# Two pairs of layer-norm statistics back to back, one square root for the first pair, late transposes moved behind the paired chunks

## The chip, the cores and the metric

The kernel runs on one core of a Trainium2 chip. The metric is device time in microseconds (us). A core has five engines with a program order each: TensorE (PE, matrix products and transposes), VectorE (DVE), ScalarE (ACT), GpSimd (POOL) and SyncE (SP, here a queue that issues transfers). Transfers run on 16 DMA engines. Engines wait for each other by semaphores.

## What is computed

Two layers, each an attention block (A) and a dense block (B), each with a residual, over 2048 tokens of width 1024, in bf16:

```python
x = A_x                                   # [1, 2048, 1024]
for _ in range(2):
    x = x + A(layernorm(x), wqkv, wo)     # 32 heads of 32; each token sees 8 tokens, 2 apart
    x = x + B(layernorm(x), w1, b1, w2, b2)   # 1024 -> 3584, gelu, -> 1024
```

Layer norm subtracts a token's mean and divides by the square root of its variance plus 1e-5.

## The kernel before

Tokens are cut into four groups of 512, a group into four tiles of 128 tokens. With two layers there are eight stages n = 0 to 7. For each stage, `gen_qkv` makes queries, keys and values, chunk by chunk (`qkv_chunk`, 8 matmuls of 128x512 for each of 8 chunks); DVE makes the products of queries and keys (`new_prod`), the softmax and the weighted values (`av`, which writes chunk c of `oT`); `gen_wo` multiplies by wo, and `gen_ffn1` and `gen_ffn2` are block B. Of `wo`, the accumulation runs over the chunks c = 0 to 7 of `oT`. PE takes its work in the order of the program. The wrapper `InOrder` (L81) does the same for another engine while its flag `on` is set: `vec` is DVE, `act` is ACT, `sp` is SP. Where the flag is off, a scheduler places the instructions.

The change lies at the very start, in stage 0. A normalised tile has to reach PE transposed (`xnT`, features on the partitions). For the first four tiles, x[0] to x[3], this goes two ways:

- Tiles 0 and 1: PE transposes the raw x (`banks[0]`, `banks[1]`; ACT copies each bank into `raw` in two parts, features k = 0, 1 first and k = 2 to 7 later). `queries_of_raw` multiplies the raw tiles by the query weights, in rows of 7 chunks for each k from 0 to 7 (matmuls of 128x258), and mean and standard deviation are worked in afterwards: `spread_stats` (after row k = 2) turns them into rows on PE, and `finish(c)` corrects each chunk. For the keys and values, the same two tiles are also normalised on DVE (`norm(0)`, `norm(1)`, list `first_early`) and transposed by DMA on the SP queue.
- Tiles 2 and 3: DVE makes statistics (`stats`: two BATCH_NORM_STATS2 and one BATCH_NORM_AGGREGATE), ACT the root (`root`), DVE the reciprocal and the normalised tile (`norm`). PE transposes them (`first_late`, `transpose_on_pe`) between the matmuls of `queries_of_raw`, both into the same PSUM bank, and ACT copies the bank to `xnT` in between.

Behind `queries_of_raw`, `gen_qkv` sends the SP queue on. In this order stand there: the two DMA transposes of `first_early`; the first half of the key weights wk, x[6], the second half of wk, x[7], x[8] to x[11]; then, tile by tile, the DMA transposes of `ln_early`, which normalises x[4] to x[9] on DVE with the root on ACT (`ln_stats` with `root=True`). x[10] and x[11] get their statistics on ACT (`ln_stats_ahead`, an Identity activation with a sum, then a Square activation with a sum, L213 and L214); here `act.on` is only set for g == 2, and the `act` wrapper keeps their order among themselves alone. The stage then needs wk for its key chunks, which DVE multiplies with the queries as they come.

Of the kernel before, what the change touches and what calls it, by code (L numbers as in the profile page):

```python
# [8 lines left out]
ACT = mybir.ActivationFunctionType  # L9
# [8 lines left out]
def kernel(  # L18
# [18 lines left out]
    P = 128  # L37
# [13 lines left out]
    KD = D // P  # L51
# [26 lines left out]
    def acc_tile():  # L78
        return psum.tile([P, T], F32, name="acc", bufs=8)
# [23 lines left out]
    vec, act, pool, sp = InOrder(nc.vector), InOrder(nc.scalar), InOrder(nc.gpsimd), InOrder(nc.sync)  # L103
# [6 lines left out]
    def pe(inst):  # L110
        if last_pe[0] is not None:
            dep_order(inst, last_pe[0], "PE program order")
        last_pe[0] = inst
        return inst

    def mm(*args, **kwargs):
        return pe(nc.tensor.matmul(*args, **kwargs))  # L117
# [37 lines left out]
    eps_t = const.tile([P, 1], F32, name="eps_t")  # L155
# [71 lines left out]
    def transpose_on_pe(xn, out, bank, parts=(0, KD)):  # L227
        pst = bank[:].bitcast(BF16).rearrange("p (k t) -> p k t", t=P)
        for k in range(KD):
            pe(nc.tensor.transpose(pst[:, k, :], xn[:, k * P:(k + 1) * P], ident[:]))  # L230
        copy_transposed(out, bank, parts)

    def copy_transposed(out, bank, parts):
        pst = bank[:].bitcast(BF16).rearrange("p (k t) -> p k t", t=P)
        for k0, k1 in zip(parts[:-1], parts[1:]):
            act.copy(out[:, k0:k1, :], pst[:, k0:k1, :])
# [8 lines left out]
    first_early, first_late = [], []  # L245
    NT = 2 * P

    def ln_first():

        xnT = xa[0] = new_xnT()  # L250
        vec.on = act.on = True
        raw = attp.tile([P, KD, NT + 2], BF16, name="vT", bufs=2)
        vec.memset(raw[:, :, NT:NT + 2], 1.0)
        mv = lnp.tile([P, 4, 2], F32, name="mvs", bufs=1)
        std = lnp.tile([P, 4], F32, name="stds", bufs=1)
        rstd = lnp.tile([P, 4], F32, name="rstds", bufs=1)
        less = lnp.tile([P, 2], F32, name="lesses", bufs=1)

        def stats(tt):
            st6 = lnp.tile([P, 2, 6], F32, name="stats")  # L260
            for h in range(2):
                vec.bn_stats(st6[:, h, :], x[tt][:, h * HALF:(h + 1) * HALF])
            vec.bn_aggr(mv[:, tt, :], st6[:])

        def root(tt):
            act.activation(std[:, tt:tt + 1], mv[:, tt, 1:2], ACT.Sqrt, bias=eps_t[:])

        def norm(tt, out):
            if tt > 1:
                vec.reciprocal(rstd[:, tt:tt + 1], std[:, tt:tt + 1])  # L270
            vec.tensor_scalar(out=out, in0=x[tt][:], scalar1=mv[:, tt, 0:1], scalar2=rstd[:, tt:tt + 1],
                              op0=ALU.subtract, op1=ALU.mult)
            return out

        warm_ps = acc_tile()
        warm_up(7, warm_ps)
        banks = [acc_tile(), acc_tile()]
        for tt in range(2):
            transpose_on_pe(x[tt], raw[:, :, tt * P:(tt + 1) * P], banks[tt], (0, 2))
        warm_up(2, warm_ps)  # L280
        stats(0)
        root(0)
        copy_transposed(raw[:, :, 0:P], banks[0], (2, KD))
        stats(1)
        root(1)
        copy_transposed(raw[:, :, P:NT], banks[1], (2, KD))
        vec.tensor_scalar(out=less[:], in0=mv[:, 0:2, 0], scalar1=-1.0, scalar2=None, op0=ALU.mult)
        vec.reciprocal(rstd[:, 0:2], std[:, 0:2])
        by_token = iop.tile([P, 4, P], F32, name="tmp")

        def spread_stats(bank):
            for i, column in enumerate((less[:, 0:1], less[:, 1:2], rstd[:, 0:1], rstd[:, 1:2])):
                pe(nc.tensor.transpose(bank[:, i * P:(i + 1) * P], column.to_broadcast([P, P]), identf[:]))
            rows = by_token[:].rearrange("p i t -> p (i t)")
            act.copy(rows, bank[:])
            return rows[:, 0:NT], rows[:, NT:2 * NT]

        xn01 = bigp.tile([P, 2, D], BF16, name="big")
        first_early.append((norm(0, xn01[:, 0, :]), xnT[:, 0, :, :]))

        def rest():
            for tt in range(2, 4):
                stats(tt)
                root(tt)
                if tt == 2:
                    first_early.append((norm(1, xn01[:, 1, :]), xnT[:, 1, :, :]))
                xn = lnp.tile([P, D], BF16, name="xn", bufs=3)
                norm(tt, xn[:])
                first_late.append((xn, xnT[:, tt, :, :]))

        return raw, spread_stats, rest

    def queries_of_raw(wq, qT):
        raw, spread_stats, rest = st.pop("raw")
        first = {}

        def row(c, k):
            if k == 0:
                first[c] = acc_tile()
            mm(first[c][:, 0:NT + 2], lhsT=wq[k // (KD // 2)][:, k % (KD // 2), c::NCH], rhs=raw[:, k, :],  # L320
               start=(k == 0), stop=(k == KD - 1), skip_group_check=True)

        part = attp.tile([P, NCH, NT], F32, name="abc")

        def finish(c):
            vec.scalar_tensor_tensor(out=part[:, c, :], in0=less, scalar=first[c][:, NT:NT + 1], in1=first[c][:, 0:NT],
                                     op0=ALU.mult, op1=ALU.add)
            pool.tensor_tensor(out=qT[:, c, 0:NT], in0=part[:, c, :], in1=rstd, op=ALU.mult)

        for k in range(KD):  # L330
            for c in range(7):
                row(c, k)
                if (k, c) == (0, 6):
                    bank = acc_tile()
                if (k, c) == (2, 6):
                    less, rstd = spread_stats(bank)
                    rest()
                if (k, c) == (5, 3):
                    transpose_on_pe(*first_late.pop(0), bank)
                if (k, c) == (7, 6):  # L340
                    transpose_on_pe(*first_late.pop(0), bank, (0, KD // 2, KD))
        act.on = False
        act.hold()
        for c in range(7):
            finish(c)
        for k in range(KD):
            row(7, k)
        vec.on = False
        return lambda: finish(7)

    def new_xnT(pool=None):
        return (pool or xnp).tile([P, NTT, KD, P], BF16, name="xnT")
# [38 lines left out]
    def gen_qkv(n, defer=False, qk_pool=None, v_late=False, qk_next=None, v_first=False, mix=0):  # L391
# [29 lines left out]
        if n == 0:  # L421
            last = queries_of_raw(wq, qT)
            for xn, out in first_early:
                sp.dma_start_transpose(out, xn.rearrange("s (k p) -> s k p", p=P))
            wk = load_qkv(1, lambda: load_x(1, 2, 3))
            load_x(1, 3, 4)
            load_x(2)
            early_tiles = ln_early((1, None), (2, qk_next))
            for tt in range(2):
                next(early_tiles)  # L430
                if tt == 0:
                    last()
            wv = load_qkv(2)
            for _ in early_tiles:
                pass
            vec.hold()
            sp.on = False
            sp.hold()
# [203 lines left out]
    def warm_up(count, ps):  # L642
        for _ in range(count):
            mm(ps[:], lhsT=warm[:], rhs=warm[:].unsqueeze(1).to_broadcast([P, NTT, P]), start=True, stop=True)
# [62 lines left out]

    pool.on = True
    st["raw"] = ln_first()
    first = build_constants()  # L710
    with tc.tile_pool(name="early", bufs=1) as early:
# [63 lines left out]
```

## Time and profile before

| | |
|---|---|
| median of 4 runs | 1229.23 us (1229.04 to 1229.52) |
| the profiled execution | 1229.28 us, span 1227.5 us |
| PE busy | 1220.2 us, 99% of the span |
| DVE / ACT / POOL busy | 865.5 / 314.6 / 121.5 us |
| granted PE clock | 1.0 |

The profile is of one execution. Its page gives busy times; a timeline gives start, length, engine, line, operation, "written<-read" and shapes, with the idle time ahead of a row and what ended it in square brackets. Neighbouring rows of one kind are merged ("x2"). Line 92 is the wrapper `InOrder`, line 117 is `mm`, so rows are told apart by their tiles: `stds` and `mvs` belong to tiles 0 to 3, `std` and `mv` to `ln_early`, `vT` is also the buffer of `raw` at the start, `big` holds the normalised tiles 0 and 1 there. PEld rows are weight loads, which run ahead of their matmuls. SPq rows are the times that the SP queue spent on issuing, not the transfer itself. The chain of waits follows the work that ended last back in time, and shows start, length and what.

### The profile page before, as it was taken

The page shows a single profiled execution, that of the slowest core. Times are in us where ns is not written, and L with a number is a line of the kernel's source. Part 1 is how long each engine was busy: PE and PEld are TensorE (multiplying, and loading weights), DVE is VectorE, ACT ScalarE, POOL GpSimd, SP SyncE. Part 2 cuts the span into 40 slices and gives each one's busy share as a digit, 9 for nine tenths or more (in the row PEclk, how much of TensorE's full clock was granted, in tenths as well). Part 3 has the DMA queues.
Part 4 walks back from the last instruction along what each step waited for, and adds up shares of the span by engine and source line. Part 5 has one row for each costly group of instructions (what it writes and reads, how often), then busy time and mean ns, then how long its engine had stood idle before and what let it go on. Part 6 is the DMA issues. An engine that isn't in the chain of part 4 may idle for free.

```text
span 1227.5 us, 13975 instructions
## 1 busy us (share of the span) xinstructions
PE 1220.2 (99%) x5719; PEld 632.0 (51%) x5769; DVE 865.5 (71%) x926; ACT 314.6 (26%) x498; POOL 121.5 (10%) x217
## 2 busy tenths in 40 slices
PE   9999999999999999999999999999999999999998
PEld 7666544456444554446544465444654444444444
DVE  7999897998898999375993759937598797011001
ACT  4443253014410243202431024310234001300310
POOL 2430006010101101100001000000000001000000
PEclk9999999999999999999999999999999999999999
DMA  9976665765738645856557565486664568446541
GB/s 309 266 220 194 181 198 174 202 186 190 226 121 254 185 151 162 238 172 172 167 158 224 172 171 185 155 218 198 171 204 148 186 191 210 149 160 193 157 136 50
DMA packets 225824, 227.18 MB, mean 185 GB/s; under 512 B 74000, under 2 KB 192928, under 8 KB 223712
## 3 DMA queue, kind: packets, MB, share of 16 engines
q1 hardware_dynamic: 216304, 208.17, 56.5%
q0 software_dynamic: 8880, 17.07, 4.2%
q8 instruction: 45, 0.74, 0.3%
q10 hardware_dynamic: 576, 1.05, 0.2%
q14 instruction: 19, 0.16, 0.0%
HBM read 189.01 MB, written 4.19 MB: 157 GB/s over the span
## 4 chain that ended last, share of the span: by engine, by line
PE 90%; DVE 7%; DMA 1%; issue 1%; SPq 0%; ACT 0%; POOL 0%; DVEq 0%
PE acc L117 90%; DVE big L92 5%; DMA x<-in_A_x_dram 1%; DVE stats L92 1%; DVE e L92 0%; DMA abc<-a 0%; DVE tmp L92 0%; DVE oT L92 0%; SPq L92 0%; POOL abc L92 0%; DVE xn L92 0%; DVE qT L92 0%; DVE a L92 0%; DVE z L92 0%; ACT vT L92 0%
## 5 line engine op out<-in xcount | busy, mean ns | idle before, releaser
L117 PE MATMUL acc<-xnT,wt 128*128 128x512 bf16 (+1 forms) x3328 | 712.9, 377 | 0.1
L117 PEld LDWEIGHTS <-wt 128*128 128x128 bf16 x3392 | 400.7, 119 | 318.8 <-issue 0.9
L117 PE MATMUL acc<-wt,hT 128*128 128x512 bf16 (+1 forms) x1780 | 386.0, 376 | 2.1
L117 PEld LDWEIGHTS <-hT 128*128 128x128 bf16 x1820 | 178.0, 98 | 209.1
L92 DVE TENSOR_TENSOR big<-big 128x2048 bf16<-128x2048 bf16 (+2 forms) x185 | 244.8, 1351 | 2.2
L92 ACT ACTIVATE hT<-acc,b1T 128x512 bf16<-128x512 f32 x224 | 151.7, 688 | 323.3 <-PE acc L117 323.2
L92 DVE TENSOR_TENSOR big<-qT,kT 128x4096 bf16<-128x4096 bf16 x64 | 143.8, 2283 | 37.4 <-ACT kT L92 35.9
L92 DVE TENSOR_TENSOR big<-abc,vT 128x4096 bf16<-128x4096 bf16 x64 | 144.6, 2282 | 11.2 <-DMA abc<-a 7.2
L92 DVE TENSOR_TENSOR tmp<-acc,b2bc 128x512 f32<-128x512 f32 x56 | 38.6, 689 | 154.0 <-PE acc L117 150.9
L92 ACT CAST qT<-acc 128x512 bf16<-128x512 f32 (+1 forms) x64 | 35.5, 558 | 275.4 <-PE acc L117 275.3
L117 PE MATMUL acc<-wt,oT 128*128 128x512 bf16 x440 | 97.5, 379 | 0.4
L92 DVE BATCH_NORM_STATS2 stats<-x 128x6 f32<-128x512 bf16 x116 | 77.3, 680 | 5.0 <-DMA x<-in_A_x_dram 4.0
L117 PEld LDWEIGHTS <-oT 128*128 128x128 bf16 x448 | 43.8, 98 | 52.9 <-issue 0.2
L92 DVE TENSOR_TENSOR x<-acc,big 128x512 bf16<-128x512 f32 (+1 forms) x9 | 5.7, 632 | 90.1 <-PE acc L117 90.0
L92 POOL TENSOR_TENSOR rstd<-mv,eps_t 128x1 f32<-128x1 f32 x48 | 14.6, 304 | 500.2 <-DVE mv L92 500.2
L92 ACT CAST vT<-acc 128x512 bf16<-128x512 f32 x64 | 37.4, 585 | 100.7 <-PE acc L117 100.7
L92 ACT CAST kT<-acc 128x512 bf16<-128x512 f32 x64 | 37.0, 584 | 59.7 <-PE acc L117 59.7
L92 DVE TENSOR_TENSOR x<-acc,x 128x512 bf16<-128x512 f32 x64 | 42.9, 670 | 5.2 <-PE acc L117 4.8
L92 DVE TENSOR_SCALAR xn<-x,mv,rstd 128x1024 bf16<-128x1024 bf16 x48 | 26.2, 545 | 19.9 <-POOL rstd L92 19.9
L92 DVE TENSOR_TENSOR x<-tmp,x 128x512 bf16<-128x512 f32 x56 | 38.6, 689 | 1.4
L92 POOL DMA_DIRECT2D big<-big x24 | 13.3, 564 | 212.3 <-DVE big L92 212.2
L92 ACT ACT_TABLE_LOAD x17 | 21.8, 1283 | 43.7 <-DVE e L92 30.7
(82 smaller groups left out, 303.4 us busy)
## 6 DMA issues: line engine op xcount, KB each, us to landing
wt<-in_B_w_dram SPq DMA_DIRECT2D x56, 1024.0 KB, 5.8
wt<-in_B_w_dram SPq DMA_DIRECT2D x64, 896.0 KB, 5.0
wt<-in_A_wqkv_dram SPq DMA_DIRECT2D x46, 1024.0 KB, 5.7
wt<-in_A_wo_dram SPq DMA_DIRECT2D x16, 1024.0 KB, 5.1
abc<-a POOLq DMA_DIRECT2D x32, 256.0 KB, 4.7
big<-big POOLq DMA_DIRECT2D x24, 256.0 KB, 3.9
out_dram<-x SPq DMA_DIRECT2D x31, 128.0 KB, 1.8
x<-in_A_x_dram SPq DMA_DIRECT2D x14, 256.0 KB, 5.9
```

Of the source, the lines that this page charges most:

```text
L92: inst = f(*args, **kwargs)
L117: return pe(nc.tensor.matmul(*args, **kwargs))
```

## The change

In ACT's order, both late parts of the raw copies now stand ahead of the roots, and one root covers tiles 0 and 1. In DVE's order, the statistics of tiles 2 and 3 follow directly on the reciprocal of tiles 0 and 1; then come norm(2), norm(3), norm(0), norm(1). On PE, the transposes of tile 2 move from behind chunk 3 of row k = 5 to the end of row k = 6; those of tile 3 stay at the end of row k = 7. The order of the SP queue is the same.

```diff
-        def root(tt):
-            act.activation(std[:, tt:tt + 1], mv[:, tt, 1:2], ACT.Sqrt, bias=eps_t[:])
+        def root(t0, t1):
+            act.activation(std[:, t0:t1], mv[:, t0:t1, 1], ACT.Sqrt, bias=eps_t[:])
...
-        stats(0)
-        root(0)
-        copy_transposed(raw[:, :, 0:P], banks[0], (2, KD))
-        stats(1)
-        root(1)
-        copy_transposed(raw[:, :, P:NT], banks[1], (2, KD))
+        for tt in range(2):
+            copy_transposed(raw[:, :, tt * P:(tt + 1) * P], banks[tt], (2, KD))
+            stats(tt)
+        root(0, 2)
...
-        first_early.append((norm(0, xn01[:, 0, :]), xnT[:, 0, :, :]))
 
         def rest():
             for tt in range(2, 4):
                 stats(tt)
-                root(tt)
-                if tt == 2:
-                    first_early.append((norm(1, xn01[:, 1, :]), xnT[:, 1, :, :]))
+                root(tt, tt + 1)
+            for tt in range(2, 4):
                 xn = lnp.tile([P, D], BF16, name="xn", bufs=3)
                 norm(tt, xn[:])
                 first_late.append((xn, xnT[:, tt, :, :]))
+            for tt in range(2):
+                first_early.append((norm(tt, xn01[:, tt, :]), xnT[:, tt, :, :]))
...
-                if (k, c) == (5, 3):
+                if (k, c) == (6, 6):
                     transpose_on_pe(*first_late.pop(0), bank)
                 if (k, c) == (7, 6):
                     transpose_on_pe(*first_late.pop(0), bank, (0, KD // 2, KD))
```

## The prediction

> **What bounds the kernel now.** I read the engine shares, the chain of waits, then the timelines of the first 30 us and of 121 to 124 us.
>
> The page's engine shares:
>
> ```profile
> PE 1220.2 (99%) x5719; PEld 632.0 (51%) x5769; DVE 865.5 (71%) x926; ACT 314.6 (26%) x498; POOL 121.5 (10%) x217
> ```
>
> TensorE (PE) is busy for 99% of the span, but that is an average. Two windows of the chain of waits say more, one up to 24 us, one around 122 us (start, length, what):
>
> ```profile
> 12.71 0.29 SPq L92
> ...
> 13.05 0.57 SPq L92
> ...
> 14.70 8.37 DMA x<-in_A_x_dram
> ...
> 23.09 1.30 DVE stats L92 x2
> ```
>
> ```profile
> 114.34 7.88 DVE big L92 x6
> 122.22 0.68 DVE oT L92 x2
> 122.90 10.79 PE acc L117 x49
> ```
>
> Until 122.90 us the chain does not run through PE. It runs through VectorE (DVE), and before 23.09 us through SyncE's DMA queue (SP): DVE waits there for x[7], issued at 14.70 and landed at 23.07. From 122.90 on, the chain is PE to the end of the span. So a delay of DVE is lost time once it exceeds DVE's slack at 122.9, and a delay of PE is lost time in full. What was the SP queue doing before 13.05?
>
> ```profile
> 8.79 4.21 SPq L92 DMA_TRANSPOSE xnT<-big  x2
> 13.05 0.57 SPq L92 DMA_DIRECT2D wt<-in_A_wqkv_dram  x1
> 13.68 0.49 SPq L92 DMA_DIRECT2D x<-in_A_x_dram  x1
> 14.22 0.43 SPq L92 DMA_DIRECT2D wt<-in_A_wqkv_dram  x1
> 35.33 2.64 SPq L92 DMA_TRANSPOSE xnT<-qT  x2
> ```
>
> The transposes of tiles 0 and 1 stand ahead of both halves of wk (13.05, 14.22) and of x[6], x[7]. They go out when norm(0) and norm(1) are done, and the change moves those two norms to the end of DVE's first block. That decides the case.
>
> **Part by part.**
>
> *Front of PE (gain).* ScalarE's (ACT) rows:
>
> ```profile
> 6.11 0.79 ACT L92 COPY vT<-acc 128x768 bf16<-128x768 bf16 x1
> 7.26 0.29 ACT L92 ACTIVATE stds<-mvs,eps_t 128x1 f32<-128x1 f32 x1 [0.36 <-DVE mvs L92]
> 7.46 0.78 ACT L92 COPY vT<-acc 128x768 bf16<-128x768 bf16 x1
> 8.29 0.93 PE L117 MATMUL acc<-vT,wt 128*128 128x258 bf16 x7 [0.30 <-ACT vT L92]
> ```
>
> Each copy stands behind a root (the first root at 5.91), and PE waits for the second. In the changed order the copies run at 5.91 to 6.70 and 6.60 to 7.38, so row k=2 starts when the 14 matmuls before it are through (6.07 + 14 x 0.11 = 7.61): 0.67 us earlier than 8.29. The paired root falls at 7.29, the reciprocal at 7.63 instead of 7.59: nothing.
>
> *Late transposes (cost on PE).* They stood 17 matmuls apart and now stand 7 apart (0.77 us), in the same bank. The ACT copy that frees the bank takes 0.99 us and starts 0.2 after the first set, so the second set waits about 0.4. With the wait of 0.16 that this place had before, PE reaches the first 128x256 query about 0.3 earlier (15.33 to 15.0).
>
> *DVE's block.* Now: reciprocal 7.63, statistics of 2 and 3, norms 2, 3, 0, 1. x[2] landed at 7.98 (issue 1.80 plus 6.2), so statistics run from 8.00, 1.28 + 0.21 each with the rows' overlaps, to 10.93. Then norm 2 from 10.99, 3 from 11.64, 0 from 12.09, 1 from 12.54 to 13.09 (0.55 each, 0.45 where one follows another, the reciprocals between). Before, the block ended at 13.81: DVE gains 0.7, of which two removed waits for a root are 0.32 + 0.36.
>
> *The SP queue (the large cost).* norm(0) ends at 12.64 instead of 8.34. The first transpose goes out at 12.69 instead of 8.79 and nothing passes it. Two of them cost at least 2 x 1.24 plus 0.05; the quiet pair at 35.33 held the queue for 2.64 and released it at 38.01, the pair at 8.79 for 4.21, because the second one took 2.78 while loads were under way. In the changed kernel no load is queued ahead of them but x[5], which landed at 13.17, so I take the quiet pair: the first half of wk goes out at 12.69 + 2.73 (35.33 to 38.06) = 15.4 instead of 13.05. Landing times in the DMA issue rows (last number, us to landing), for the loads at 14.22, 38.06 and 118.34 (the one at 13.05 has 5.9):
>
> ```profile
> wt<-in_A_wqkv_dram SPq DMA_DIRECT2D x1, 1024.0 KB, 8.2
> wt<-in_A_wqkv_dram SPq DMA_DIRECT2D x1, 1024.0 KB, 5.7
> wt<-in_A_wo_dram SPq DMA_DIRECT2D x1, 1024.0 KB, 5.0
> ```
>
> After a quiet pair it is 5.7: its first half lands at 15.4 + 5.7 = 21.1 instead of 13.05 + 5.9 = 19.0, and everything behind it in the queue keeps its distance. So the delay d of wk's second half and of x[7] is 2.1. Bounds: 1.3 (nothing under 5.0 us is seen for 1 MB, and the queue cannot be free before 15.2) and 3.7 (the second transpose takes 2.78 again). I take 2.1, because the pair at 35.33 is the nearest row: two transposes, then 1 MB loads, nothing large in flight ahead of them.
>
> *What d does to PE.* wk's second half lands at 22.4, needed by the fifth matmul of the first key chunk: queries from 15.33, 64 x 0.109, then 4 x 0.216 = 23.17. Slack 0.75. With d = 2.1 it lands at 24.5: PE stands still about 1.7 us and is 1.4 later than before from there; the 0.3 gained at the front is swallowed.
>
> *What d does to DVE.* x[7]'s statistics start at 25.2 instead of 23.09: 2.1 later. The 0.7 gained is swallowed by the same wait.
>
> *One more instruction on ACT.* Outside the edit, the scheduler places one root differently. In the changed program's order, the Square activation of x[10] (from ln_stats_ahead, L214) stands ahead of the root of tile x[9]; now it stands behind:
>
> ```profile
> 28.33 0.19 ACT L92 ACTIVATION_READ_ACCUMULATOR xn<-x 128x1 f32 x1
> 28.75 0.29 ACT L92 ACTIVATE std<-mv,eps_t 128x1 f32<-128x1 f32 x1 [0.23 <-DVE std L92]
> 28.95 1.14 ACT L92 ACTIVATE xn<-x,less 128x1024 bf16<-128x1024 bf16 x1
> ```
>
> With ACT's earlier roots also 2.1 later (26.70 to 28.80), the chain is root 0.2, kT cast 0.47, sum 0.96, read 0.22, Square 1.06, read 0.09: the root starts at 31.8, ends at 32.1. DVE's reciprocal wants it at 29.24 + 2.1 = 31.34. Cost 0.8 on DVE; bounds 0 (ACT caught up) and 1.2 (all of Square plus its read). DVE is then 2.9 late, and its block of products up to 122.9 runs without a gap that could take this back: its one wait after that, 1.99 before 88.61, is for weights that DVE itself makes.
>
> *Where both meet.* wo's first chunk needs oT of c = 7, written at 122.90; PE loads those weights at 123.82 (load at 123.39 is the sixth, plus 2 x 0.215). DVE slack 0.9. PE alone asks for +1.4; DVE for 2.9 - 0.9 = 2.0. They run side by side, so the later one counts: +2.0. Behind it the chain is PE alone, with nothing to win back.
>
> Sum: 1229.28 (profiled execution: span 1227.5 plus 1.8 around it; the median is 1229.23, 0.05 below) + 2.0 = 1231.3.
>
> *A rule on standing still.* The profile's PEclk row shows full clock in every slice, and no wait of PE after 4.3 us exceeds 0.5; mine are 1.7 at 23 us and 0.6 at 123. At the very start the row of warm-up matmuls shows 7 in 3.17 us, 0.427 apart, twice the later 0.216. If a stop of 1.7 brought that back for such a stretch, PE would lose half of 3.2, 1.6 more, and be at +3.0 instead of +2.0.
> The Trainium skill, "TensorE: Matmul & The Clock Gate", Part 1 ("What's actually happening"), puts the fall to half clock at an idle window of about 3.4 us; by that rule a stop of 1.7 costs nothing more and the sum stays +2.0.
>
> **Rivals.** 0.2% is 2.46 us, about what a measurement of this kernel can tell from no change.
>
> (1) *The transpose pair stays slow.* If it holds the queue for 4.21, d is 3.7: DVE 3.7 + 0.8 - 0.9 = +3.6, PE 3.7 - 0.75 = +2.95, time 1232.9. For it: four of the five pairs in the first 50 us that I looked at have a slow second transpose. Against: in each of these a load was in flight ahead. It passes 0.2% from d = 2.6.
>
> (2) *Half clock after the stop*: +3.0, 1232.3, as above.
>
> (3) *ACT catches up*: no 0.8; PE's +1.4 decides, 1230.7.
>
> (4) *Not slower.* The loads land when they did: then PE keeps its 0.3 and DVE its 0.7, and the time is 1229.0. It needs d below 0.6, against the queue's own times (15.2 at the earliest, against 13.05), and what it wins is under 0.2% all the same. A gain over 0.2% has no row behind it: PE's waits before 14 us add up to 1.3.
>
> **Numbers.** Forecast (+1.6 to +2.46) 0.38; (3) and other mild cases, d down to 1.3, 0.16; (4) 0.04; (1) 0.22; (2) 0.07; a further late transfer that I do not see, slower, 0.11; faster by over 0.2%, 0.02. So faster 0.02, same 0.58, slower 0.40. Range: low end d = 1.3 without ACT's cost, where PE decides with 1.3 - 0.75 = +0.55, less the 0.25 by which the runs shown lie off their middle; high end rival (1) with the same 0.1 to 0.2 more: 1229.6 to 1233.0.
>
> **What would show it.** First transpose on SP near 12.7, wk's halves issued near 15.4 and 16.5; PE waiting 1.7 near 22.9 for a wt landing; DVE waiting 2 to 4 us in all for x[6] and x[7], statistics of x[7] near 25.2; root of x[9] near 31.8 behind Square; PE waiting about 0.6 for oT near 125. It is wrong if wk goes out before 14.5 or after 17, if PE does not wait for oT, or if a wait after 126 us has grown.

## The result, and the profile after

| | before | changed |
|---|---|---|
| median | 1229.19 us (51 runs, 1228.88 to 1229.57) | 1231.33 us (31 runs, 1230.76 to 1233.60) |
| profiled execution | 1229.28 us, span 1227.5 | 1233.36 us, span 1231.6 |
| mean granted PE clock in it | 1.000 | 0.998 |

The ratio is 1.002 (95% interval 1.0015 to 1.0025): 2.14 us or 0.17% slower, under the 2.46 us that the prediction set as the bound for "no change that a measurement of this kernel can tell"; the interval leaves no doubt that it is slower. The forecast was 1231.3.

The times of the changed kernel lie in two groups. 24 of the 31 are at 1230.76 to 1231.87, with a granted clock of 1.000; 7 are at 1232.80 to 1233.60, with 0.998 or 0.999. The profiled execution belongs to the upper group, so it shows more than the median holds; the experiment `again` below gives a trace of the lower group.

The engine shares of the changed kernel say as little as those before: PE 99%, DVE 70%.

```profile
PE 1222.2 (99%) x5719; PEld 632.7 (51%) x5769; DVE 865.4 (70%) x926; ACT 314.8 (26%) x497; POOL 117.7 (10%) x217
```

The chain of waits of the changed kernel, from the end of DVE's block on (start, length, what):

```profile
12.30 0.92 DVE big L92 x2
13.21 2.78 DVE abc L92 x7
15.99 0.13 SPq L92
...
16.17 0.58 SPq L92
...
17.38 8.11 DMA wt<-in_A_wqkv_dram
25.48 0.05 issue
```

Before, the chain went from the SP queue to x[7] and on along DVE up to 122.9 us. Now it goes from norms 0 and 1 (`big`, 12.30) over the SP queue to the second half of wk, issued at 17.38 and landed at 25.48, and from 25.53 us on it is PE alone. (The row `abc` at 13.21 lies beside the two transposes, which held SP until 16.12.) The SP queue itself, in the timeline:

```profile
12.78 3.34 SPq L92 DMA_TRANSPOSE xnT<-big  x2
16.17 0.58 SPq L92 DMA_DIRECT2D wt<-in_A_wqkv_dram  x1
16.80 0.53 SPq L92 DMA_DIRECT2D x<-in_A_x_dram  x1
17.38 0.43 SPq L92 DMA_DIRECT2D wt<-in_A_wqkv_dram  x1
```

The pair goes out at 12.78 instead of 8.79, the halves of wk at 16.17 and 17.38 instead of 13.05 and 14.22. The engines that need the data follow, PE's timeline first, then DVE's (in brackets the idle time ahead and what ended it):

```profile
15.41 8.01 PE L117 MATMUL acc<-xnT,wt 128*128 128x256 bf16 x68
25.53 4.71 PE L117 MATMUL acc<-xnT,wt 128*128 128x512 bf16 x13 [2.11 <-DMA wt<-in_A_wqkv_dram]
```

```profile
22.80 1.29 DVE L92 BATCH_NORM_STATS2 stats<-x 128x6 f32<-128x512 bf16 x2 [2.99 <-DMA x<-in_A_x_dram]
26.18 1.29 DVE L92 BATCH_NORM_STATS2 stats<-x 128x6 f32<-128x512 bf16 x2 [1.24 <-DMA x<-in_A_x_dram]
33.19 0.16 DVE L92 RECIPROCAL std<-std 128x1 f32<-128x1 f32 x1 [0.78 <-ACT std L92]
```

PE waits 2.11 us for the second half of wk: the fifth matmul of the first key chunk starts at 25.53 instead of 23.18. DVE is 3.1 later at x[7] (26.18 against 23.09) and waits 0.78 for the root of x[9]. Behind the stop, the windows view shows what parts the two groups (columns: window, its length, busy time and count of PE, PEld, DVE, ACT, POOL, granted clock, DMA share, GB/s):

```profile
23.20:25.60 2.40, 0.29 (x3) 0.07 (x2) 1.67 (x5) 0.83 (x3) 0.00 (x0) 1.00 1.04 387
26.18:29.59 3.41, 3.41 (x10) 1.34 (x8) 3.30 (x8) 0.77 (x2) 0.00 (x0) 0.50 1.17 299
29.59:33.00 3.41, 3.41 (x17) 2.26 (x16) 2.72 (x8) 3.17 (x7) 0.23 (x1) 1.00 1.03 268
```

For 3.41 us the granted clock is 0.50, and PE makes 10 matmuls there instead of 17. The first wo matmul, at 122.46 before, starts at 126.56: 2.35 of the 4.1 are the stop; half of 3.41, 1.7, is the clock.

### The profile page after: what moved, and what is told of

The parts are those of the page before. It is cut to its first block, busy times and chain, and to the rows that moved or that the text cites. A ratio compares the mean times of both kernels' runs of the same rounds, so it can differ in the third digit from the quotient of the medians.

```text
span 1231.6 us, 13974 instructions
## 1 busy us (share of the span) xinstructions
PE 1222.2 (99%) x5719; PEld 632.7 (51%) x5769; DVE 865.4 (70%) x926; ACT 314.8 (26%) x497; POOL 117.7 (10%) x217
## 4 chain that ended last, share of the span: by engine, by line
PE 98%; DMA 1%; DVE 1%; issue 0%; ACT 0%; SPq 0%
PE acc L117 97%; DMA wt<-in_A_wqkv_dram 1%; DMA x<-in_A_x_dram 0%; DVE abc L92 0%; DVE stats L92 0%; ACT vT L92 0%; PE acc L230 0%; SPq L92 0%; DVE xn L92 0%; DVE big L92 0%; DVE x L92 0%; DVE mvs L92 0%; DVE rstds L92 0%; ACT stds L92 0%
```

## The experiments

The question was which of the late things sets the time: PE's stop for wk, DVE's delay with the root of x[9], or the half clock; and whether the early part of the change gains anything. Each group of runs had its own runs of the kernel before beside it: at 1229.01 us for `again`, `wk_ahead`, `norms_back` and `only_norms_late`, at 1229.17 for `only_front`, `wk_ahead_apart`, `root_first` and `filled_stop`, at 1229.16 for `late_moved`, `four_ahead` and `one_ahead`. Differences are against these.

**The changed kernel once more** (`again`), no edit.

> The changed kernel unaltered, for a second trace and more times. Theory (a stop of PE at the fifth matmul of the first key chunk, sometimes followed by 3.4 us of half clock): times in two groups, about 1231.0 to 1231.9 and 1232.8 to 1233.6, at most one in three in the upper; a trace from the lower group has full clock throughout, the same order of events as the first one, the first transpose issued at 12.7 to 12.8 and wk's second half landing 2 to 3.1 us later than in the kernel before (22.4). Rival (all of the loss comes later, from oT arriving late at wo): a trace of the lower group shows PE waiting more at 123 to 127 us than at 23 to 25.

Measured: 1231.26 us (11 runs, 1230.56 to 1232.13), ratio 1.0018 (1.0009 to 1.0027), +2.25. None of the 11 is in the upper group. The profiled execution (1231.71) has full clock throughout. Its SP queue sends the pair at 12.64 and wk at 15.55 and 16.73; the second half lands at 24.83. The stop and the same stretch behind it, from PE's timeline and the windows view:

```profile
24.88 5.40 PE L117 MATMUL acc<-xnT,wt 128*128 128x512 bf16 x24 [1.48 <-DMA wt<-in_A_wqkv_dram]
```

```profile
26.18:29.59 3.41, 3.41 (x17) 2.27 (x16) 3.27 (x10) 1.21 (x4) 0.00 (x0) 1.00 1.20 275
```

The fifth matmul of the key chunk is 1.70 later than before, the first wo matmul 2.35 later. Between them stands one more wait, in PE's timeline and in the chain of waits:

```profile
60.00 5.19 PE L117 MATMUL acc<-xnT,wt 128*128 128x512 bf16 x23 [0.37 <-DMA wt<-in_A_wqkv_dram]
```

```profile
24.88 16.64 PE acc L117 x76
...
52.18 1.78 SPq L92
...
54.06 5.89 DMA wt<-in_A_wqkv_dram
...
60.00 65.19 PE acc L117 x301
```

The next stage's wk is issued at 54.06 (before: 49.90), behind late transposes on the same queue, and costs PE 0.53 in all. Those transposes carry tiles that DVE normalises, the second at 49.43 here and at 46.21 before, and the pair held the queue for 4.43 instead of 3.48. So by the chain this part of the loss does come over DVE and the queue. At wo it does not: there, the last oT is written at 124.78 and PE loads those weights at 126.22. DVE has 1.4 to spare, though its products started 3.2 late. The wait that gave this back is the one for the softmax weights (`abc<-a`), before and in `again`:

```profile
88.61 4.49 DVE L92 TENSOR_TENSOR big<-abc,vT 128x4096 bf16<-128x4096 bf16 x2 [1.99 <-DMA abc<-a]
```

```profile
90.49 4.49 DVE L92 TENSOR_TENSOR big<-abc,vT 128x4096 bf16<-128x4096 bf16 x2 [0.66 <-DMA abc<-a]
```

**wk ahead of the transposes** (`wk_ahead`), from the changed kernel:

```diff
-            for xn, out in first_early:
-                sp.dma_start_transpose(out, xn.rearrange("s (k p) -> s k p", p=P))
-            wk = load_qkv(1, lambda: load_x(1, 2, 3))
+            def transposes():
+                for xn, out in first_early:
+                    sp.dma_start_transpose(out, xn.rearrange("s (k p) -> s k p", p=P))
+                load_x(1, 2, 3)
+            wk = load_qkv(1, transposes)
```

> Changed kernel with one move on the SP queue: the first half of wk goes out ahead of the two DMA transposes of tiles 0 and 1 instead of behind them; DVE, ACT and PE edits stay as changed. Queue theory: wk's first half is issued near 8.7 and lands near 16, the transposes go out at 12.7 as before, the second half of wk and x[7] land near 22 to 23, so PE's stop at 23 us is under 0.5 us and DVE's waits shrink by 2 to 3 us: 1228.7 to 1229.6. Rival (DVE's new order itself is what makes it late): 1230.5 to 1231.5 as the changed kernel.

Measured: 1229.29 us (11 runs), ratio 1.0002 (0.9993 to 1.001), +0.28. The SP timeline shows the first half of wk at 8.59 and the second at 16.95, landed at 22.74:

```profile
8.59 0.46 SPq L92 DMA_DIRECT2D wt<-in_A_wqkv_dram  x1
12.55 3.72 SPq L92 DMA_TRANSPOSE xnT<-big  x2
16.95 0.43 SPq L92 DMA_DIRECT2D wt<-in_A_wqkv_dram  x1
```

PE has no stop, and 2.0 of the 2.25 us are gone with every engine order of the change in place. So the loss lies in the order of the SP queue. This run does not part PE's delay from DVE's, since x[7] comes earlier with wk: its statistics start at 23.44, 0.35 later than before, where they are 2.4 later in `again`. No run of it lies beyond 1229.69.

**The norms back where they were** (`norms_back`): norm(0) behind the reciprocal of the pair, norm(1) behind the statistics of tile 2; everything else of the change stays.

```diff
+        first_early.append((norm(0, xn01[:, 0, :]), xnT[:, 0, :, :]))
         def rest():
             for tt in range(2, 4):
                 stats(tt)
                 root(tt, tt + 1)
+                if tt == 2:
+                    first_early.append((norm(1, xn01[:, 1, :]), xnT[:, 1, :, :]))
...
-            for tt in range(2):
-                first_early.append((norm(tt, xn01[:, tt, :]), xnT[:, tt, :, :]))
```

> Changed kernel, but norm(0) follows the reciprocal again and norm(1) the statistics of tile 2, as in the kernel before; paired root, copies first and the late transposes behind rows 6 and 7 stay. Queue theory (the loss is the late DMA transposes holding wk and x[6], x[7]): first transpose issued at 8.2 to 8.8, wk's first half at about 13, PE does not stop at 23 us, all of the loss gone: 1228.7 to 1229.3, no runs near 1233. Rival (the late PE transposes, both in one bank and 7 matmuls apart, are what costs): the loss stays, 1230.5 to 1231.5.

Measured: 1229.64 us (11 runs), ratio 1.0004 (0.9995 to 1.0013), +0.63. wk goes out at 12.81, its second half lands at 22.23, and the stop is gone. The time is above the expected range: PE's two sets of late transposes wait 0.36 and 0.48, and the first query starts at 15.68 instead of 15.33. Of these 0.35, 0.26 were there already at the first row of the raw queries (6.33 against 6.07), so the rise is not explained by the transposes alone.

**Only the norms late** (`only_norms_late`), from the kernel before: the front, the roots and the transposes on PE as they were.

```diff
-        first_early.append((norm(0, xn01[:, 0, :]), xnT[:, 0, :, :]))
...
-                if tt == 2:
-                    first_early.append((norm(1, xn01[:, 1, :]), xnT[:, 1, :, :]))
...
+            for tt in range(2):
+                first_early.append((norm(tt, xn01[:, tt, :]), xnT[:, tt, :, :]))
```

> The kernel before with one edit: norm(0) and norm(1) moved behind norm(2) and norm(3); single roots, copies between the roots and the late transposes at their old places. Queue theory: the first transpose goes out at about 14.3 (norm(3) ends at 13.8 there, plus 0.5), later than the 12.8 of the changed kernel, so the delay is 4 to 5 us and the kernel is slower than the changed one: 1232 to 1234.5. Rival (loss from the late PE transposes): 1229.0 to 1229.5.

Measured: 1232.53 us (6 runs, 1231.81 to 1233.75), ratio 1.003 (1.0018 to 1.0041), +3.52. Here the first transpose goes out at 14.20, the second half of wk lands at 25.87 and PE stands 2.1 us. This one move is more than the whole loss. The rest of the change (statistics earlier, one root) takes 1.3 of it back, or 1.0 when the runs at full clock alone are compared. It ends DVE's block earlier, so that the first transpose goes out at 12.64 in `again`; that this is what gives the time back is argued, not tested apart. Two of the six runs, at 1233.75 both, had a granted clock under 1.

**Only the front** (`only_front`), from the kernel before: copies ahead of the roots and one root for the pair; norms and late transposes as before.

```diff
-        stats(0)
-        root(0)
-        copy_transposed(raw[:, :, 0:P], banks[0], (2, KD))
-        stats(1)
-        root(1)
-        copy_transposed(raw[:, :, P:NT], banks[1], (2, KD))
+        for tt in range(2):
+            copy_transposed(raw[:, :, tt * P:(tt + 1) * P], banks[tt], (2, KD))
+            stats(tt)
+        root(0, 2)
```

> The kernel before with the first part of the change alone: both late copies of the raw tiles ahead of the roots, one root for tiles 0 and 1; norms and late transposes where they were. By the prediction's term PE comes 0.3 to 0.7 earlier at row k = 2, but the late transposes of tile 2 at row 5 then wait for the normalised tile, ready at about 11.3 to 11.6 us: PE is at the first query within 0.2 of before, time 1228.8 to 1229.3. Rival (one root for both costs DVE a wait of 0.5 to 0.9 for the pair, as the second trace shows, and all later tiles follow it): 1229.4 to 1229.9.

Measured: 1229.20 us (11 runs), ratio 1.0 (0.9991 to 1.0009), +0.03. In its trace PE reaches the first query at 14.91 and the first wo matmul at 122.05, 0.4 earlier than before both times (0.1 of it at the first row of the raw queries, 5.97 against 6.07), and that execution (1228.94) is 0.34 shorter than the profiled one of before. The medians don't show it, and with an interval of 1.1 us to either side they could not: a gain of 0.4 at the front stays undecided.

**Only the late transposes moved** (`late_moved`), from the kernel before:

```diff
-                if (k, c) == (5, 3):
+                if (k, c) == (6, 6):
```

> The kernel before with the PE transposes of tile 2 moved from row 5 to the end of row 6, nothing else. The prediction's term: the second set waits for the bank about 0.4 to 0.5 instead of 0.16, so PE is 0.3 late at the first query; this lies on PE's path, unless the key chunk's slack takes it: 1229.2 to 1229.6. Rival (the set's place costs nothing): 1229.0 to 1229.2, as the kernel before.

Measured: 1229.43 us (11 runs), ratio 1.0003 (0.9994 to 1.0012), +0.27. The second set waits 0.48 for its bank, and the first query starts at 15.80, 0.47 later:

```profile
14.45 0.61 PE L230 MATMUL acc<-ident,xn 128*128 128x128 bf16 x8 [0.32 <-ACT xnT L92]
```

(The bracket counts from the modelled end of the matmul before it; start to start, PE lost 0.48.) Not all of the 0.47 is the move. The rows of mean and deviation (`spread_stats`) already start 0.16 late here, at 9.22 against 9.06; from them to the first query it is 6.58 against 6.27, so the move costs 0.31.

**wk ahead, and the transposes apart** (`wk_ahead_apart`): `wk_ahead` with `(6, 2)` in place of `(6, 6)`, so that the bank is free in time. If PE's earlier start were worth anything by itself, this version would beat both kernels.

> The variant with wk's first half ahead of the transposes, and the PE transposes of tile 2 moved from the end of row 6 to behind its third chunk, so that 11 matmuls (1.2 us) lie between the two sets instead of 7 (0.77): the ACT copy that frees the bank (1.0 plus 0.2) fits between. If the bank is what the second set waits for (0.49 in the traces), PE reaches the queries 0.4 earlier than in that variant: 1228.6 to 1229.1, unless wk's second half (landed at 22.7) then ends the wait, which takes 0.2 to 0.4 back. Rival (the wait is for the normalised tile 3): no change, 1229.1 to 1229.5.

Measured: 1229.41 us (11 runs), ratio 1.0002 (0.9993 to 1.0011), +0.24: missed. The bank wait fell from 0.49 to 0.04 and the first query started at 14.71, but then PE waited for the second half of wk, which landed at 23.18:

```profile
14.71 8.01 PE L117 MATMUL acc<-xnT,wt 128*128 128x256 bf16 x68
23.23 4.11 PE L117 MATMUL acc<-xnT,wt 128*128 128x512 bf16 x18 [0.51 <-DMA wt<-in_A_wqkv_dram]
```

The fifth key matmul starts at 23.23, before at 23.18. What PE gains at the front, it gives back at this place.

**wk late without any other edit** (`four_ahead` and `one_ahead`), from the kernel before: loads of x put ahead of wk in the SP queue, all of x[8] to x[11] or x[8] alone.

```diff
             for xn, out in first_early:
                 sp.dma_start_transpose(out, xn.rearrange("s (k p) -> s k p", p=P))
+            load_x(2)
             wk = load_qkv(1, lambda: load_x(1, 2, 3))
             load_x(1, 3, 4)
-            load_x(2)
```

```diff
+            load_x(2, 0, 1)
             wk = load_qkv(1, lambda: load_x(1, 2, 3))
             load_x(1, 3, 4)
-            load_x(2)
+            load_x(2, 1)
```

> The kernel before with one move on the SP queue: the loads of x[8] to x[11] (four of 256 KB, 0.68 us each in the traces) go out ahead of wk instead of behind x[7]. No engine's instructions change, only wk, x[6] and x[7] land later. Queue theory with the slack of 0.75 at the fifth matmul of key chunk 0: d = 4 x 0.68 = 2.7, PE stops there for about 2.0 and the kernel is 2.0 to 2.6 slower: 1231.0 to 1231.8, with some runs near 1233 (half clock after the stop). Rival (the changed kernel is slow for its order on DVE, ACT and PE): 1229.0 to 1229.6.

> The same with one load, x[8], ahead of wk: d = 0.68. Queue theory: it just fits into the slack of 0.75, so PE does not stop at the key chunk: 1229.0 to 1229.5. Rival (loss in proportion to the delay, no slack): 0.6 slower, 1229.7 to 1229.9.

As in the changed kernel, x[6] and x[7] come later with wk. Measured: `one_ahead` 1229.37 us (11 runs), ratio 1.0001 (0.9992 to 1.001), +0.21. The second half of wk lands 0.8 later, at 23.19, and the fifth key matmul starts at 23.24, 0.06 later: the slack of 0.75 is there. `four_ahead` 1234.44 us (5 runs, 1232.08 to 1235.12), ratio 1.0036 (1.0023 to 1.005): all five lie above the expected range. The delay there was 4.2, more than the expected 2.7, and why is open; the two runs with a granted clock of 1.000 are at +2.9 and +3.6, the three with 0.997 to 0.999 at +5.3 to +6.0. The delay d of wk against the loss, runs at full clock alone:

| | second half of wk landed | d | d - 0.75 | measured |
|---|---|---|---|---|
| `one_ahead` | 23.19 | 0.8 | 0.05 | +0.2 |
| `again` | 24.83 | 2.4 | 1.7 | +2.25 |
| `only_norms_late` | 25.87 | 3.5 | 2.7 | +2.8 to +3.5 |
| `four_ahead` | 26.60 | 4.2 | 3.5 | +2.9, +3.6 |

From 0.6 us below to 0.8 above, the loss is d less the slack (d is from the one profiled execution of each, and for the last two rows that execution had a half clock; the loss is from the timed ones).

**The root of x[9] first** (`root_first`), from the changed kernel: the Square of x[10] has to stand behind the root of x[9], as in the kernel before.

```diff
-            act.activation(junk[:], x[t][:], ACT.Square, bias=less[:], accum_out=var)
+            square = act.activation(junk[:], x[t][:], ACT.Square, bias=less[:], accum_out=var)
+            if g == 2 and tt == t0:
+                dep_order(square, last_root[0], "root first")   # last_root: set in ln_stats
```

> Changed kernel with one order pinned: the root of x[9] on ACT ahead of the Square activation of x[10], as in the kernel before. The prediction's step (0.8 us on DVE, and DVE decides at wo): lower group 0.6 faster, median near 1230.7. Theory after the second trace (DVE ends 1.4 us early at wo, because the transfer of the softmax weights gives back what DVE lost; PE's own stop decides): median unchanged within 0.2, 1231.1 to 1231.5.

Measured: 1231.12 us (11 runs), ratio 1.0018 (1.0009 to 1.0027), +1.95. The rows are in the order of before again, ACT's first and then DVE's:

```profile
31.22 0.29 ACT L92 ACTIVATE std<-mv,eps_t 128x1 f32<-128x1 f32 x1 [0.23 <-DVE std L92]
31.42 1.13 ACT L92 ACTIVATE xn<-x,less 128x1024 bf16<-128x1024 bf16 x1
```

```profile
31.71 0.16 DVE L92 RECIPROCAL std<-std 128x1 f32<-128x1 f32 x1
31.91 0.55 DVE L92 TENSOR_SCALAR qT<-x,mv,std 128x1024 bf16<-128x1024 bf16 x1
32.37 4.49 DVE L92 TENSOR_TENSOR big<-qT,kT 128x4096 bf16<-128x4096 bf16 x2
```

The reciprocal no longer waits, and the products start at 32.37 instead of 33.11 in `again`. The time is 1231.12 against 1231.26; each against its own runs of before, 0.30 less. That is short of the 0.6 that the prediction's sum asks for, but with 1.1 us to either side the times alone do not exclude it. The trace says more: the last oT is written at 125.03, no earlier than in `again`, because the softmax weights made DVE wait 1.63 here, and PE loads it 0.9 later still, at 125.97. So in both traces DVE does not hold PE at wo. One of the 11 runs, at 1233.51, had a granted clock of 0.999.

**The stop filled** (`filled_stop`), from the changed kernel: six matmuls of 128x512 on spare data between the two halves of the first key chunk; their results are not used. In this program the scheduler also put the root of x[9] ahead of the Square.

```diff
-            ps = qkv_chunk(wk, c, xnT)
+            if n == 0 and c == 0:
+                spare = acc_tile()
+                ps = qkv_chunk(wk, c, xnT, k1=KD // 2)
+                warm_up(6, spare)
+                qkv_chunk(wk, c, xnT, ps=ps, k0=KD // 2)
+            else:
+                ps = qkv_chunk(wk, c, xnT)
```

> Changed kernel with six matmuls of the warm-up kind (1.3 us) into a spare bank, between the two halves of key chunk 0, where PE stands still for 1.5 to 2.1 us. The output is the same. Clock theory (the upper group of times, 1232.8 to 1233.6, is the stop at 23 us followed by half clock): PE is idle for under 1 us there, no run is above 1232.3, the median stays at 1231.0 to 1231.6, because the matmuls fit into the stop. Rival (the upper group comes from transfers that land later in some runs): 1 to 3 of the 11 runs are still above 1232.5. The build also moves the root of x[9] ahead of Square; by the prediction's step this alone would give up to 0.6 back.

Measured: 1231.40 us (11 runs, 1230.78 to 1231.67), ratio 1.0018 (1.0009 to 1.0026), +2.23. PE's timeline shows the six in the place of the stop, and the clock is full:

```profile
23.21 1.46 PE L117 MATMUL acc<-big 128*128 128x512 bf16 x6
24.66 6.70 PE L117 MATMUL acc<-xnT,wt 128*128 128x512 bf16 x30
```

The time is that of the lower group, so at full clock the stop costs its length and no more that these times could tell. None of the 11 lies in the upper group, but neither did any of `again`; the counts alone do not show that filling the stop keeps the clock. The record of the granted clock says more about where half clock comes from. Full clock begins in the changed kernel's trace at 5.70 us, and 26.18 is 5.70 plus six times 3.413. The window of 3.41 us ahead of it, 22.76 to 26.18, holds the whole stop of 2.27. The other two traces with half clock have the same shape, `only_norms_late` and then `four_ahead` (windows view):

```profile
27.24:30.65 3.41, 3.41 (x9) 1.32 (x8) 3.27 (x10) 1.25 (x4) 0.00 (x0) 0.50 1.19 283
```

```profile
24.58:27.98 3.40, 1.34 (x6) 0.93 (x7) 1.80 (x6) 0.83 (x3) 0.00 (x0) 1.00 1.36 153
28.00:31.40 3.40, 3.40 (x10) 1.31 (x8) 3.26 (x10) 1.27 (x4) 0.00 (x0) 0.50 1.06 289
```

In each, half clock lasts one window of 3.41 and follows a window with about 2.1 to 2.3 us of standing in it, counted from where the next matmul would have started (in `four_ahead`, 3.40 less 1.34). In `again`, where a window's boundary cuts the stop of 1.64 and no window holds more than 1.37 of it, the clock stays full. The ends of the runs, where PE's work thins out, narrow it further. By the windows view (length less PE's busy time) PE stood 1.66 in the window 1222.62 to 1226.03 of the kernel before and 1.63 in 1224.99 to 1228.40 of `again`, and no half clock followed; the three windows that half clock did follow have 1.93 to 2.11 by the same count.

## Why the prediction was right

- *What bounds the kernel*: that the SP queue decides the case was right, and the experiments show it from both sides: with wk ahead of the transposes or with the norms in their old place at most 0.63 us is left, inside the interval of the measurement; the late norms alone cost more than the whole change.
- *The SP queue*: the first transpose went out at 12.78 and 12.64, predicted 12.69. The pair did not take the quiet 2.64 but 3.34 and 2.86: the first transpose took 2.00 and 1.5, where I had 1.24 to 1.33. Why is open; in `root_first`, `filled_stop` and `only_norms_late` the pair took 2.71 to 2.76, so the quiet pair was the right row and the profiled execution of the changed kernel the odd one. wk went out at 16.17 and 15.55, not 15.4, and d was 3.1 and 2.4, not 2.1. Rival (1), the pair at 4.21 and d = 3.7, did not come.
- *Front of PE*: the predicted 0.3 earlier at the first query was 0.1 later in the trace (15.41; before 15.33), but the two terms were right. From the first row of the raw queries to the rows of mean and deviation it is 2.35 instead of 2.99, a gain of 0.64 (predicted 0.67), and from there to the first query 6.59 instead of 6.27, a loss of 0.32. What is missing in the sum is that the first row itself started at 6.47 instead of 6.07: the clock record shows full clock from 5.70 us on, in the kernel before from 4.06, and the 16 transposes of x ahead of that row took 1.72 instead of 1.28. `again` has the same picture, with full clock from 6.43 and the row at 6.48. The reciprocal came at 8.04 instead of the predicted 7.63 for the same reason, since its root now stands behind copies that wait for these transposes; in `only_front` and `wk_ahead`, with full clock from 4.8 and 4.7, it came at 7.55 and 7.54. None of it reaches the time, since the wait for wk swallows it, as the prediction said of the 0.3.
- *One more instruction on ACT*: predicted 0.8, measured 0.78, in the place that was named. It does not count at wo, where DVE had time to spare with it (`again`) and without it (`root_first`).
- *Where both meet*: this is the step that failed. PE was to be held by oT at wo, with DVE 2.0 behind its slack. The prediction names "if PE does not wait for oT" as a sign that it is wrong, and PE did not wait for oT in either trace of this kernel. In `again` DVE starts its products 3.2 late and writes the last oT 1.9 late, and PE is 2.35 late by then, so oT is 1.4 ahead of its use. I had written that DVE's block had no gap to take a delay back, because the 1.99 before 88.61 is a wait for weights that DVE itself makes. That wait has a second part, their transfer: it took 4.2 to 4.5 us from issue to landing before and 2.8 to 3.2 in `again`, which gave 1.3 back. In the profiled execution of the changed kernel it took 4.5 to 4.8, and gave nothing back; even there oT (127.21) was ahead of PE's load of it (127.90), but only since the half clock had put PE 1.7 back. With a transfer that long and full clock DVE could bind after all; no trace of this kernel has the two together. Why this transfer is shorter at one time than at another is open.
- *The sum*: PE's term was put at +1.4 and was +1.70 at the fifth matmul in `again`, +2.35 at wo, with 0.53 from the wk of the next stage and 0.1 of smaller waits. I had looked for no wait between 30 and 122 us. The two errors offset: a PE term that was 0.9 too small and a DVE term of +2.0 that bound in neither trace. That the total of +2.0 lies so near the measured +2.14 is luck; its working is not what happened.
- *Half clock after the stop*, rival (2), at a chance of 0.07: it happened in 8 of the changed kernel's 32 executions (the profiled one and 7 timed ones) and in none of the 11 of `again`, the same program. Its price was put at 1.6 on a stop of 1.7; the profiled execution shows 1.7, and the two groups lie 1.9 apart (middles 1233.1 and 1231.2). The rule that I set against it (the Trainium skill, "TensorE: Matmul & The Clock Gate", Part 1, "What's actually happening": half clock after an idle window of about 3.4 us) does not hold as I read it: stops of 2.1 to 2.3 us within one window were enough here. The price was right. It came in too few executions to move the median.
- *Rival (3)*, ACT catches up and PE decides, named the right engine for the wrong reason: in `again` PE decides at wo, with ACT's 0.8 in place.
- *Rival (4)*, loads landing when they did: `norms_back` and `wk_ahead` are that case, at +0.63 and +0.28 where I had -0.2. No gain of the front arrives even then: in `norms_back` the two sets of late transposes cost 0.73 against the 0.64 that the front gains, and in `wk_ahead_apart` the first query is 0.6 earlier and the fifth key matmul is where it was.

Still open: the 0.5 us beyond d - 0.75 in `again`. It is a wait at 59 us in `again`, which comes over DVE and the SP queue, and a wait of 0.41 for wo's second half in `root_first`; a third trace, `filled_stop`, has neither. That the SP queue still runs late then is argued from the trace; no run took such a wait away by itself.

## What to carry to other kernels

When a step is moved on one engine, follow what it issues into the queue and list what stands behind it there: here moving two norms of 0.45 us by some 4 us put two weight loads 2.4 to 3.1 us late, and taking the first of these loads out from behind them undid nearly all of it. A block that "runs without a gap" may still give time back if one of its waits is for a transfer, so a sum that depends on two engines meeting later needs the slack of each measured there. A sum that comes out right is not yet right in its terms; taking away a part of the term that is said to decide (`root_first`), and reading the slack where the two engines meet, showed that it didn't.

## What the runs showed of the hardware

- Half clock did not need a long stop: 1.93 to 2.11 us of standing (a window's length less PE's busy time) within one window of 3.41 us, counted from where full clock begins, was followed by exactly one window (3.41 us) at 0.50; 1.37 us in a window was not, nor 1.63 and 1.66 at the ends of two runs. The start of that count differed from run to run (4.1 to 7.0 us), and so did the length of the stop (2.27 and 1.64 in the two traces of the changed kernel). Either can be why the same program has half clock in some executions and not in others; no run parts them.
- The first DMA transpose of the pair (128x1024, from SBUF) held the SP queue for 1.5 us in one execution of the changed kernel and for 2.00 in another; the second took 1.24 in both.
- The transfer of the softmax weights took from 2.8 to 4.8 us in executions of programs that differ by nothing in that part.
